# Reordering the first stretch of a fused attention and mixture kernel: who stores the head outputs, whose VectorE steps go first, how PSUM pairs rotate, and what is stored of the first expert's weights

## The chip, the cores and the metric

The kernel runs on one core of a Trainium2 chip. A core has a matrix engine (TensorE, PE in the profile; its weight loads are PEld), VectorE (DVE), ScalarE (ACT), GpSimd (POOL) and SyncE (SP), which here only issues DMA transfers. ScalarE can issue transfers too. Each engine executes its own instructions in order and waits on semaphores for the others. TensorE writes to eight PSUM banks of 128 x 512 floats; VectorE and ScalarE read them from there[...].

The time is the device time of the core in microseconds (us), from the first to the last instruction. All data is 32-bit float.

## The reference

First a causal linear attention with decay, 4 batches, 8 heads, 768 positions, head size 64. In blocks, for every head with its decay `lam`:

```python
intra = einsum('bhic,bhjc->bhij', qb, kb) * Dmask      # lam ** (i - j), lower triangle
intra = einsum('bhij,bhjd->bhid', intra, vb)
inter = einsum('bhid,bhde->bhie', qb * lam_pow, kv_state)
out[:, :, sl] = intra + inter
kv_state = lam_block * kv_state + einsum('bhsd,bhse->bhde', kb * rev_pow, vb)
```

The result, with the heads side by side, is x: 3072 tokens of width 512. Then four experts (512 to 1024 to 512), each token's outputs weighted by its normalised domain probabilities:

```python
p = domain_probs / (domain_probs.sum(-1, keepdims=True) + 1e-09)
for e in range(4):
    h = maximum(x @ w1[e], 0.0)
    out += p[:, e:e + 1] * (h @ w2[e])
```

## The kernel before

**Attention.** The sequence is cut into 24 chunks of 128 positions (six for each batch, all eight heads together). A chunk passes three steps of TensorE work, each with a pair of PSUM banks:

- `turn` (L494) transposes q and k (L500). ScalarE copies both out (qT L505, kT L506), VectorE makes qs, the decayed q, and GpSimd decays k in place for the state (`decayed`, kn in the profile).
- `scores` (L514) multiplies q and k of all heads (sp, L520). VectorE masks the two banks with the decays (two st of 128 x 512).
- `values` (L534) makes the outputs: from the state (L546, not in a batch's first chunk), from the masked scores (L551), and the new state's addend (L559, not in the last). ScalarE copies the outputs out (xc, L567), VectorE updates the state kv.

They are skewed: in turn i stand turn(i), scores(i-1), values(i-2). The pair of banks is chosen by the chunk's number modulo 3 (`pairs[n % 3]`), so all three steps of a chunk share a pair. `load` fetches q and k of four chunks ahead and v of three, in transfers of 128 and 256 KB whose rows are 64 floats.

**Experts.** Tokens are taken in three groups of 1024. Both matrix products of an expert use the Strassen-Winograd scheme: seven products of half-sized blocks (M1 to M7) in the place of eight, with sums of blocks as operands. For x times w1 it is nested: each of the seven products is done by seven inner ones. An inner product (L817, tile pg) is two 128x128 by 128x256 matmuls, four records in the profile; ScalarE or VectorE adds it up, and VectorE makes the sums hS of the hidden blocks for the second product (L871). A pair of group and expert is a unit; the seven products go in the order SEQ = M1, M5, M6, M2, M7, M3, M4. After the first unit's x-w1 part, TensorE interleaves the second product of one unit with the first of the next.

An operand tile of w1 is `ws_in`: 128 x 7 x 256 floats, four blocks and three further sums of them made by four GpSimd steps. There are two such buffers. For later use the operands of each expert are kept in DRAM: `w1_ops`, 896 KB for each of the seven products (`prepare_w1`, `inner`), and sums of w2 in `w2_sums` (`prepare_w2`). The x operands are `xs`: for the first group they stay in SBUF; for the other two the attention stage stores them to DRAM (`x_blocks`), both the plain head outputs (L574) and the block sums that GpSimd makes of a chunk and the one four before (`pair_sums`, tile to, L607).

**The first stretch**, which the change touches. `DENSE` = 14 turns of attention run alone; between them a list of chores (`chores`, started one at a time by `pump` when an estimate of GpSimd's load allows) fetches and completes the first expert's operands M1 and M5 (`own_fill`, `own_inner`, `own_sum`) and makes the w2 sums of expert 0. Then `first_product` does the seven products of the first unit; after each inner product `rest` gives VectorE one step from `background`, and `attend` issues attention steps at a rate (the rest spread over 35 inner steps). `own_fill` of the next product is called before a product begins; for S1 and S2 it is a ScalarE copy, for S3 and S4 two GpSimd subtractions, else a load. `own_inner` also stores each finished operand tile in five transfers, for the use of expert 0 in groups two and three.

Where the order comes from: `soon` puts attention's VectorE steps (qs, st, kv) in front of `background`, newest first; `values` settles those it still needs. A stored head output goes to the list `late` and is issued by SP two slots on; `store` does the like for GpSimd's results once its estimated load is through. SP's transfers are issued in the order of the program, and each waits for its data and for its buffer. In the program's semaphores a transfer also waits for the one eight before it in program order, whichever engine issued it.

```python
        if dense[0]:
            settle_up(what)
        else:
            background[0:0] = work
```

The functions below stand with the line numbers of the profile.

Of the kernel before, what the change touches and what calls it, by code (L numbers as in the profile page):

```python
# [22 lines left out]
def kernel(  # L23
# [11 lines left out]
    nc = tc.nc  # L35
# [289 lines left out]
    def own_fill(m):  # L325
        t = own[m] = stream.tile([P, 7, 256], FP32, name="ws_in", tag="w")
        a, blk = A_OF[m], whole(t)
        if a == "S3":
            halves(blk, raw["A11"][:], raw["A21"][:], ALU.subtract)
        elif a == "S4":  # L330
            halves(blk, raw["A12"][:], raw["S1"][:], ALU.subtract)
        elif a in ("S1", "S2"):
            nc.scalar.copy(out=blk, in_=raw["S1"][:])
        else:
            i, j = int(a[1]) - 1, int(a[2]) - 1
            nc.sync.dma_start(
                out=blk, in_=moe_w1[0, j * 256:(j + 1) * 256, i * W:(i + 1) * W].rearrange("(c p) f -> p c f", p=P),
            )

    def own_inner(m):  # L340
        t = own[m]
        for to, x, y, op in ((4, 0, 1, ALU.subtract), (1, 1, 3, ALU.add), (5, 1, 0, ALU.subtract), (6, 2, 5, ALU.subtract)):
            tt(nc.gpsimd, t[:, to], t[:, x], t[:, y], op)
        to = w1_ops[0, MS.index(m)]
        store(lambda: (
            nc.sync.dma_start(out=to[:, 0], in_=t[:, 0]),
            nc.sync.dma_start(out=to[:, 1:3], in_=t[:, 4:6]),
            nc.sync.dma_start(out=to[:, 3], in_=t[:, 1]),
            nc.sync.dma_start(out=to[:, 4], in_=t[:, 6]),
            nc.sync.dma_start(out=to[:, 5:7], in_=t[:, 2:4]),  # L350
            made.add(("w1", 0, m)),
        ))
        fed[0, 0, m] = {i: t[:, OWN_AT[i]] for i in OWN_AT}

    def own_sum(name):
        if name == "S1":
            raw["S1"] = stage.tile([P, 2, W], FP32, name="w1o", tag="st")
            halves(raw["S1"][:], raw["A21"][:], raw["A22"][:], ALU.add)
        else:
            halves(raw["S1"][:], raw["S1"][:], raw["A11"][:], ALU.subtract)  # L360
# [5 lines left out]
    for n, names in ((0, "qk"), (1, "qk"), (0, "v"), (2, "qk"), (1, "v"), (3, "qk"), (2, "v"), (3, "v")):  # L366
# [70 lines left out]
    background = []  # L437
    aside = []
# [26 lines left out]
    def soon(what, *work):  # L465
# [14 lines left out]
        else:  # L480
            background[0:0] = work
# [12 lines left out]
    def turn(n, tags):  # L494
# [39 lines left out]
    def values(n, tags):  # L534
# [37 lines left out]
        if g > 0:  # L572
            for r, m in plain.items():
                late.append((now[0] + 2, lambda r=r, m=m: nc.sync.dma_start(  # L574
                    out=x_blocks[g - 1, MS.index(m), :, :, at],
                    in_=x[:, r * 256:(r + 1) * 256].rearrange("p (a t) -> p a t", a=2),
                )))
# [37 lines left out]
    pairs = (("s0", "s1"), ("q01", "q02"), ("q11", "q12"))  # L615
# [6 lines left out]

    def attend():
# [453 lines left out]
    def nested_product(e, m, tags):  # L1077
# [45 lines left out]
    chores.extend((  # L1123
        lambda: (own_fill("M1"), raw_w1("A21", "A22")), pause(4),
# [158 lines left out]
```

## Time and profile before

The time is 1253.81 us, the median of two runs (1253.25 and 1254.37). The profiled execution spans 1251.8 us.

| engine | busy, us | share of the span | instructions |
|---|---|---|---|
| PE | 1197.9 | 96% | 6595 |
| PEld | 1036.8 | 83% | 6595 |
| DVE | 784.3 | 63% | 1330 |
| ACT | 286.7 | 23% | 522 |
| POOL | 630.4 | 50% | 628 |

The chain of work that ended last is 90% PE. Means of single steps, in the first 226 us: a mask st 682 ns, qs 862, an addition of an inner product 686, a decay kn 1087 on GpSimd, a head sum `to` 911 to 953, an operand step on ws_in 791; afterwards GpSimd's operand steps take about 0.72 us.

How to read it: a busy PE is not PE at its peak, because matmuls overlap and their ends are modelled. A mean over the span hides that the kernel has stretches with different limits, so the tables by stretch and the waits in one stretch count for more than the page's shares. The idle time of an engine that no one waits for costs nothing. The releaser of a wait is inferred; where the named one had long been done, it was another.

### The profile page before, as it was taken

To read this page: it belongs to the slowest core of one execution; us is meant where nothing else is said; L and a number is where in the kernel's file an instruction comes from. 1 tells how busy PE (TensorE), PEld (TensorE's weight loads), DVE (VectorE), ACT (ScalarE), POOL (GpSimd) and SP (SyncE) were. 2 spreads that over 40 slices of the span, in tenths; PEclk is the share of its full clock that TensorE was granted. 3 is DMA by queue.
4 is the path that set the end of the run, shared out by engine and by line. 5 is a ranking of instruction groups with operands and counts; after the bars stand their busy time and mean duration, and the time that the engine had idled before them with its cause. 6 is when DMAs were issued, how large, how long until landed. Compare 5 with 4: busy or idle time off the path is not lost.

```text
span 1251.8 us, 17937 instructions
## 1 busy us (share of the span) xinstructions
PE 1197.9 (96%) x6595; PEld 1036.8 (83%) x6595; DVE 784.3 (63%) x1330; ACT 286.7 (23%) x522; POOL 630.4 (50%) x628
## 2 busy tenths in 40 slices
PE   7888885999999999999999999999999999999998
PEld 6666663888888888888888888888888888888887
DVE  4744457278478467476476575575556566776775
ACT  3333222102102102012012022022124342242232
POOL 3468429757365422000721621467387486593784
PEclk9889989999999999999999999999999999999999
DMA  9978816987979644345675775767666535445442
GB/s 227 262 209 229 239 54 222 321 294 237 297 273 312 233 144 172 112 136 186 198 233 184 213 232 185 234 223 269 225 214 206 189 125 188 146 153 184 138 183 68
DMA packets 232390, 255.01 MB, mean 204 GB/s; under 512 B 95056, under 2 KB 185712, under 8 KB 232304
## 3 DMA queue, kind: packets, MB, share of 16 engines
q1 hardware_dynamic: 221696, 251.06, 62.9%
q10 hardware_dynamic: 10608, 2.82, 1.0%
q8 instruction: 52, 0.85, 0.3%
q14 instruction: 34, 0.28, 0.1%
HBM read 180.41 MB, written 73.42 MB: 203 GB/s over the span
## 4 chain that ended last, share of the span: by engine, by line
PE 90%; DVE 3%; DMA 2%; SPq 2%; POOL 1%; issue 1%; ACT 0%; ACTq 0%; DVEq 0%; POOLq 0%
PE pg L817 40%; PE q L871 31%; PE pq L1097 12%; PE op L551 2%; PE sp L520 2%; SPq L111 1%; PE kp L500 1%; PE op L546 1%; DVE st L76 1%; PE op L559 1%; DVE kv L76 0%; DVE m L76 0%; DVE sums L76 0%; DMA w_sums<-w2o 0%; PE qp L500 0%
## 5 line engine op out<-in xcount | busy, mean ns | idle before, releaser
L817 PE MATMUL pg<-xs,ws_in 128*128 128x256 f32 x2352 | 572.1, 382 | 14.7 <-DMA ws_in<-w_ops 10.3
L817 PEld LDWEIGHTS pg<-xs,ws_in 128*128 128x128 f32 x2352 | 445.5, 191 | 81.9 <-issue 11.3
L76 DVE TENSOR_TENSOR m<-pg,m 128x512 f32<-128x512 f32 x492 | 336.8, 688 | 146.9 <-PE pg L817 137.8
L871 PE MATMUL q<-w2t,hS 128*128 128x256 f32 x1024 | 241.9, 379 | 0.0
L871 PEld LDWEIGHTS q<-w2t,hS 128*128 128x128 f32 x1024 | 194.6, 190 | 26.5
L887 DVE SCALAR_TENSOR_TENSOR acc<-q,gate,acc 128x256 f32<-128x256 f32 x192 | 92.5, 482 | 160.3 <-PE q L871 160.0
L871 PE MATMUL q<-w2t,m 128*128 128x256 f32 x768 | 181.9, 379 | 0.3 <-DMA w2t<-in_moe_w_dram 0.2
L829 ACT ACTIVATE m<-m 128x512 f32<-128x512 f32 x144 | 90.7, 630 | 346.9 <-DVE m L76 346.7
L871 PEld LDWEIGHTS q<-w2t,m 128*128 128x128 f32 x768 | 146.0, 190 | 21.0 <-DMA w2t<-in_moe_w_dram 0.6
L76 POOL TENSOR_TENSOR ops<-w2b 128x256 f32<-128x256 f32 x24 | 16.9, 727 | 191.6 <-DMA w2b<-in_moe_w_dram 191.6
L76 POOL TENSOR_TENSOR m<-m,s_decay 128x512 f32<-128x512 f32 x64 | 80.4, 1273 | 63.0 <-ACT m L829 47.6
L76 POOL TENSOR_TENSOR xs<-xs 128x256 f32<-128x256 f32 x76 | 58.0, 764 | 107.2 <-DMA xs<-x_blocks 95.9
L825 ACT COPY m<-pg 128x512 f32<-128x512 f32 x96 | 56.2, 585 | 212.3 <-PE pg L817 192.2
L76 DVE TENSOR_TENSOR sums<-pq,sums 128x256 f32<-128x256 f32 x153 | 64.2, 422 | 46.0 <-PE pq L1097 35.8
L1097 PE MATMUL pq<-acc,w2t 128*128 128x256 f32 x352 | 86.6, 379 | 0.0
L1097 PEld LDWEIGHTS pq<-acc,w2t 128*128 128x128 f32 x352 | 66.8, 190 | 9.3 <-issue 0.3
L76 POOL TENSOR_TENSOR w2o<-w2b 128x512 f32<-128x512 f32 x32 | 41.5, 1317 | 59.4 <-DMA w2b<-in_moe_w_dram 21.7
L760 ACT ACTIVATE m<-m 128x512 f32<-128x512 f32 x48 | 30.3, 630 | 130.9 <-DVE m L76 130.9
L76 DVE TENSOR_TENSOR hS<-m,m 128x512 f32<-128x512 f32 x64 | 50.3, 786 | 15.4 <-ACT m L829 15.3
L76 POOL TENSOR_TENSOR acc<-hT,hT 128x512 f32<-128x512 f32 x32 | 40.3, 1272 | 30.1 <-PE pq L1097 28.2
L76 DVE TENSOR_TENSOR m<-m,m 128x512 f32<-128x512 f32 x64 | 53.6, 841 | 0.0
L76 POOL TENSOR_TENSOR acc<-hT,acc 128x512 f32<-128x512 f32 x32 | 40.6, 1270 | 7.4 <-PE pq L1097 5.4
(110 smaller groups left out, 1132.7 us busy)
## 6 DMA issues: line engine op xcount, KB each, us to landing
ws_in<-w_ops SPq DMA_DIRECT2D x77, 896.0 KB, 6.4
w2t<-w_ops SPq DMA_DIRECT2D x66, 256.0 KB, 5.0
w2t<-w_sums SPq DMA_DIRECT2D x64, 256.0 KB, 3.1
w2t<-in_moe_w_dram SPq DMA_DIRECT2D x48, 256.0 KB, 3.0
w_ops<-ops SPq DMA_DIRECT2D x21, 512.0 KB, 7.1
w1b<-in_moe_w_dram SPq DMA_DIRECT2D x16, 512.0 KB, 8.1
w2b<-in_moe_w_dram SPq DMA_DIRECT2D x32, 256.0 KB, 6.0
w_sums<-w2o SPq DMA_DIRECT2D x16, 512.0 KB, 8.8
```

The costliest lines, as they stand in the source:

```text
L76: eng.tensor_tensor(out=o, in0=a, in1=b, op=op)
L111: by.dma_start(out=to[:, :, r], in_=of[:, :, r])
L500: nc.tensor.transpose(out=x[:, ac * C:(ac + 1) * C], in_=y[:, 2 * ac:2 * ac + 2].rearrange("p r d -> p (r d)"), identity=ident[:],)
L520: nc.tensor.matmul(out=sp[r][:, ac * C:(ac + 1) * C], lhsT=hc(kT)[half[r], ac], rhs=hc(qT)[half[r], ac], start=True, stop=True,)
L551: nc.tensor.matmul(out=op[r][half[x], a * C:(a + 1) * C], lhsT=vn[:, 4 * r + 2 * a + x], rhs=hc(st[r])[:, 2 * a + x], start=(first and a = ...
L760: nc.scalar.activation(out=o[:], in_=o[:], func=AF.Relu)
L817: nc.tensor.matmul(out=p[:, j * 256:(j + 1) * 256], lhsT=ws[i][:, j * P:(j + 1) * P], rhs=xs[i], start=(fresh and j == 0), stop=True, skip ...
L825: nc.scalar.copy(out=new[at][:], in_=p[:])
L829: nc.scalar.activation(out=new[at][:], in_=new[at][:], func=AF.Relu)
L871: nc.tensor.matmul(out=p[:, s * DH:(s + 1) * DH], lhsT=h[A_OF[m]][:, c * 256 + s * P:c * 256 + (s + 1) * P], rhs=fed2[g, e, m][uu][:, c], ...
L887: nc.vector.scalar_tensor_tensor(out=o, in0=x, scalar=w, in1=o, op0=ALU.mult, op1=ALU.add)
L1097: nc.tensor.matmul(out=p[:, 0:256], lhsT=fed3[e, m, x // 2][:, x % 2, c * P:(c + 1) * P], rhs=b[B_OF[i]][:, c * 256:(c + 1) * 256], start= ...
```

## The change

Nothing of what is computed changes. Six edits belong together; they reorder the first stretch (attention and the first unit), and are meant to take waits out of it: transfers out of SP's queue, GpSimd's and VectorE's work out of the way of what TensorE needs next.

1. Head outputs of groups two and three are stored by ScalarE's queue, right after its copies, and no longer by SP two slots later.
2. Attention's VectorE steps go to a list of their own, `urgent`, taken oldest first, two after each inner product and one after each attention step, before the step from `background`.
3. PSUM pairs go round by step and not by chunk: four pairs while attention runs alone (the fourth is the one that the products use later), three afterwards. q and k are loaded five chunks ahead, v four.
4. The chores of the dense stage become a fixed table by turn (`early`); w1 blocks are fetched one at a time in turns 2 to 5; w2's sums of expert 0 move behind the dense stage, and `prepare_w1(1)` starts at the second product. Of the x operands of group one, VectorE now makes M1, M5 and M3 (before M1 and M2).
5. The first expert's w1 operands are not stored when they are made; `prepare_w1(0)` makes and stores them at the end of the list of chores, in time for group two. S3 and S4 are made in place in the raw blocks and copied by ScalarE like S1 and S2. `own_fill` of the next product comes after the first inner product, `own_inner` after the fifth.
6. A chunk's k is decayed in `scores`, one step later. The remaining attention is spread over 40 inner steps.

```diff
-        if a == "S3":
-            halves(blk, raw["A11"][:], raw["A21"][:], ALU.subtract)
-        elif a == "S4":
-            halves(blk, raw["A12"][:], raw["S1"][:], ALU.subtract)
-        elif a in ("S1", "S2"):
-            nc.scalar.copy(out=blk, in_=raw["S1"][:])
+        if a[0] == "S":
+            nc.scalar.copy(out=blk, in_=raw[{"S1": "S1", "S2": "S1", "S3": "A21", "S4": "A12"}[a]][:])
...
-        to = w1_ops[0, MS.index(m)]
-        store(lambda: (
-            nc.sync.dma_start(out=to[:, 0], in_=t[:, 0]),
...
-            made.add(("w1", 0, m)),
-        ))
...
-    for n, names in ((0, "qk"), (1, "qk"), (0, "v"), (2, "qk"), (1, "v"), (3, "qk"), (2, "v"), (3, "v")):
+    for n, names in ((0, "qk"), (1, "qk"), (0, "v"), (2, "qk"), (1, "v"), (3, "qk"), (2, "v"), (3, "v"), (4, "qk")):
...
-            background[0:0] = work
+            urgent.extend(work)
...
-        if n % NCH < NCH - 1:
-            decayed(kn)
 
     def scores(n, tags):
         qT, kT, _ = turned[n]
+        if n % NCH < NCH - 1:
+            decayed(nat[n, "k"])
...
-                late.append((now[0] + 2, lambda r=r, m=m: nc.sync.dma_start(
+                nc.scalar.dma_start(
...
-    pairs = (("s0", "s1"), ("q01", "q02"), ("q11", "q12"))
+    pairs = (("s0", "s1"), ("q01", "q02"), ("q11", "q12"), ("g1", "g3"))
...
-        f(n, pairs[n % 3])
+        f(n, pairs[next(turns) % (4 if dense[0] else 3)])
         if not attention or attention[0][0] != i:
+            if i + 5 < NT and i >= 0:
+                load(i + 5, "qk")
             if i + 4 < NT:
-                load(i + 4, "qk")
-            if 4 <= i + 3 < NT:
-                load(i + 3, "v")
+                load(i + 4, "v")
...
-    chores.extend((
-        lambda: (own_fill("M1"), raw_w1("A21", "A22")), pause(4),
-        lambda: own_inner("M1"), lambda: own_sum("S1"), lambda: (own_fill("M5"), raw_w1("A11")),
-        lambda: own_inner("M5"), lambda: own_sum("S2"),
-        *prepare_w2(0),
-    ))
+    early = {
+        2: (lambda: own_fill("M1"),), 3: (lambda: raw_w1("A21"),), 4: (lambda: raw_w1("A22"), lambda: own_inner("M1")),
+        5: (lambda: raw_w1("A11"),), 6: (lambda: own_sum("S1"),),
+        7: (lambda: own_fill("M5"), lambda: own_inner("M5")), 8: (lambda: own_sum("S2"),), 9: (lambda: own_sum("S3"),),
+        10: (lambda: x_inner(0, "M1", nc.vector), lambda: x_inner(0, "M6", nc.gpsimd), gates),
+        11: (lambda: x_inner(0, "M5", nc.vector), lambda: x_inner(0, "M2", nc.gpsimd)),
+        12: (lambda: x_inner(0, "M7", nc.gpsimd), lambda: x_inner(0, "M3", nc.vector)),
+        13: (lambda: x_inner(0, "M4", nc.gpsimd),),
+    }
...
-    rate = len(attention) / 35
+    rate = len(attention) / 40
...
-        if i > 0 and i < len(SEQ) - 1:
-            nxt = SEQ[i + 1]
-            own_fill(nxt)
-            chores.insert(0, lambda nxt=nxt: own_inner(nxt))
-            if nxt == "M2":
-                raw_w1("A12")
-            if nxt == "M7":
-                chores.extend(prepare_w1(1))
-        for f in first_product(0, 0, m, blocks, ("g1", "g3")):
+        if i == 0:
+            chores.extend(prepare_w2(0))
+        if i == 1:
+            chores.extend(prepare_w1(1))
+        for x, f in enumerate(first_product(0, 0, m, blocks, ("g1", "g3"))):
             f()
+            if 0 < i < len(SEQ) - 1:
+                if x == 0:
+                    own_fill(SEQ[i + 1])
+                    if i == 2:
+                        raw_w1("A12")
+                if x == 4:
+                    own_inner(SEQ[i + 1])
+                if i == 3 and x == 2:
+                    own_sum("S4")
             now[0] += 1
+            for _ in range(2):
+                take(urgent)
             rest()
             pump()
             credit += rate
             while credit >= 1 and attention:
                 credit -= 1
                 attend()
+                take(urgent)
...
-    chores.extend(prepare_w2(1) + prepare_w1(2) + prepare_w2(2) + prepare_w1(3) + prepare_w2(3))
+    chores.extend(prepare_w2(1) + prepare_w1(2) + prepare_w2(2) + prepare_w1(3) + prepare_w2(3) + prepare_w1(0))
```

More of the change, by code (lines that the diff above doesn't have):

```diff
@@ L343, in own_inner @@
             tt(nc.gpsimd, t[:, to], t[:, x], t[:, y], op)
-        to = w1_ops[0, MS.index(m)]
-        store(lambda: (
-            nc.sync.dma_start(out=to[:, 0], in_=t[:, 0]),
[L347 to L350, printed above, removed]
-            made.add(("w1", 0, m)),
-        ))
         fed[0, 0, m] = {i: t[:, OWN_AT[i]] for i in OWN_AT}
@@ L358, in own_sum @@
             halves(raw["S1"][:], raw["A21"][:], raw["A22"][:], ALU.add)
+        elif name == "S2":
+            halves(raw["S1"][:], raw["S1"][:], raw["A11"][:], ALU.subtract)
+        elif name == "S3":
+            halves(raw["A21"][:], raw["A11"][:], raw["A21"][:], ALU.subtract)
         else:
-            halves(raw["S1"][:], raw["S1"][:], raw["A11"][:], ALU.subtract)
+            halves(raw["A12"][:], raw["A12"][:], raw["S1"][:], ALU.subtract)
     fed = {}
@@ L437 @@
     background = []
+    urgent = []
     aside = []
@@ L573, in values @@
             for r, m in plain.items():
-                late.append((now[0] + 2, lambda r=r, m=m: nc.sync.dma_start(
+                nc.scalar.dma_start(
                     out=x_blocks[g - 1, MS.index(m), :, :, at],
                     in_=x[:, r * 256:(r + 1) * 256].rearrange("p (a t) -> p a t", a=2),
-                )))
+                )
         if not last:
@@ L621 @@
     ]
+    turns = itertools.count()
     def attend():
         i, f, n = attention.pop(0)
-        f(n, pairs[n % 3])
+        f(n, pairs[next(turns) % (4 if dense[0] else 3)])
         if not attention or attention[0][0] != i:
+            if i + 5 < NT and i >= 0:
+                load(i + 5, "qk")
             if i + 4 < NT:
-                load(i + 4, "qk")
-            if 4 <= i + 3 < NT:
-                load(i + 3, "v")
+                load(i + 4, "v")
         return i
@@ L1138 @@
             nc.scalar.dma_start(out=probs[:], in_=moe_domain_probs.rearrange("(t p) e -> p t e", p=P))
-        if i == 8:
-            gates()
-        if i > 9:
-            for m in SEQ[2 * (i - 10):2 * (i - 9)]:
-                x_inner(0, m, nc.vector if m in ("M1", "M2") else nc.gpsimd)
+        for f in early.get(i, ()):
+            f()
     dense[0] = False
-    for m in SEQ:
-        if ("x", 0, m) not in made:
-            x_inner(0, m, nc.gpsimd)
     blocks, credit = {}, 0.0
-    rate = len(attention) / 35
+    rate = len(attention) / 40
     for i, m in enumerate(SEQ):
@@ L1172 @@
                 attend()
+                take(urgent)
     while attention:
         attend()
+    while urgent:
+        take(urgent)
     fill3 = [(e, m, k) for e in range(E) for m in SEQ3 for k in range(4)]
```

## The prediction

> **What bounds the kernel now.** I read the page's slices first, then a table of stretches, then the waits of TensorE in the first 226 us, then the chain of work around the one long gap.
>
> ```profile
> ## 2 busy tenths in 40 slices
> PE   7888885999999999999999999999999999999998
>
> ```
>
> One digit is 31.3 us. From the eighth slice on TensorE is full; whatever can be won lies in the first seven. The stretches, cut at the first expert product (86.5), at the end of its last product (208.2) and at the restart (221):
>
> ```profile
> core 0: us, PE busy (x) PEld busy (x) DVE busy (x) ACT busy (x) POOL busy (x), PEclk, DMA share, GB/s
> 0.00:86.50 86.50, 66.49 (x863) 55.90 (x863) 50.92 (x101) 29.50 (x65) 37.85 (x42) 0.88 0.92 232
> 86.50:208.20 121.70, 102.36 (x966) 78.49 (x964) 68.86 (x109) 34.86 (x70) 73.28 (x83) 0.96 0.65 183
> 208.20:221.00 12.80, 2.25 (x9) 1.35 (x8) 4.30 (x5) 1.18 (x2) 12.41 (x14) 0.75 0.77 246
> 406.00:497.00 91.00, 91.00 (x423) 80.10 (x423) 57.92 (x96) 14.85 (x25) 26.75 (x30) 1.00 0.53 183
> ```
>
> From 221 a unit takes 91 us with TensorE busy for all of it: 1031 us that this change cannot shorten, only disturb. Before 221 no engine is full. At full clock the work of TensorE there is: transposes 0.44 for four, 48 fours, 21 us; scores 24 x 1.09 = 26; values 24 x 1.02 + 20 x (0.60 + 0.48) = 46; 49 inner products x 0.87 = 43; together 136 of 221 us. So 85 us are gaps, clock and operations measured longer than their best.
>
> ```profile
> PE pg L817 <- DMA ws_in<-w_ops: 10.3, 1, 10.3
> PE kp L500 <- DVE kv L76: 9.1, 11, 1.6
> PE op L546 <- DVE st L76: 7.8, 6, 1.7
> PE qp L500 <- DMA vn<-in_v_dram: 7.7, 1, 7.7
> PE op L559 <- POOL kn L76: 5.3, 1, 5.3
> PE kp L500 <- DVE kv L581: 2.8, 3, 1.7
> ```
>
> (total, times, longest). Three kinds: long single gaps, and two small ones that repeat each chunk. The 7.7 (23.1 to 30.8) has two causes: chunk 5's loads stand behind three 512 KB w1 loads in SP's order, and ScalarE, which must empty the PSUM banks, stands 8.6 us at the copy of S1 (L333) for GpSimd's sum. The 5.3 at 74.4: GpSimd waited 17.4 us for a store of w2 sums before it could reach the chunk's kn. The 10.3 is the end of this chain:
>
> ```profile
> 188.92 4.49 DMA ws_in<-in_moe_w_dram
> ...
> 199.10 3.46 POOL to L76 x3
> ...
> 206.33 4.85 DMA w2t<-in_moe_w_dram
> 211.19 4.46 DMA w_ops<-w1b
> 215.78 5.14 DMA ws_in<-w_ops
> ```
>
> M4's operand is fetched when M7 has freed its buffer, GpSimd completes it, then makes the last head sums, only then expert 1's first operand; that is stored and read back, and TensorE waits.
>
> **What the Trainium skill says.** "TensorE: Matmul & The Clock Gate", section HAM oscillation: idle gaps over some 3.4 us drop the clock to half. The trace agrees: after the 7.7 us gap the mean granted clock is 0.62 in 30.8 to 39, and a score step takes 2.01 instead of 1.09. "Perfetto Trace Analysis", section Matmuls: independent groups should rotate through PSUM banks so that evacuation overlaps; the 14 waits of kp for kv are the lack of this. "DMA: Bandwidth & Descriptors", section Issuing engines are not separate DMA queues: another issuing engine saves issue time only. The DMA share of 0.92 with 232 GB/s to 86.5 says the same: moving stores does not make room. "GPSIMD Engine Reference", section 1, Specifications: its SBUF interfaces are shared with VectorE where that reads two SBUF inputs. Here such a VectorE step takes 0.42 alone and 1.28 beside a GpSimd step.
>
> **The change part by part.**
>
> *w1 operands of expert 0 not stored, w2 sums after the dense stage, w1 blocks fetched in turns 2 to 5.* In the dense stage this takes out 1.8 MB of stores and some 2 MB of w2 loads and more of w2 sums. At 205 GB/s (the mean of 187 and 222 in the first two stretches of 10 us) chunk 5's q and k, now 4.2 MB into the queue instead of 5.8, land at 20.5 us, before TensorE asks at 23. The S1 copy comes three turns later than before, behind a sum already made. Gain: the 7.7, and the slow clock behind it (qp, kp, sp, op took 5.2 instead of 2.9: 2.3). The store that held GpSimd moves out: gain the 5.3 and its slow clock (qp, kp, sp at 4.1 instead of 2.0: 2.1).
>
> *Four PSUM pairs, taken by turn.* A turn no longer takes the pair that values has just left. That removes kp's waits: 3.8 + 1.7 before 86.5, 5.3 + 1.0 after. In the dense stage VectorE is nearly full at chunks 4 to 7 (9.73 of 10 us at 50 to 60, with qs, two st, kv and four head sums: 4.5 to 5.6 us per turn against 4.1 of TensorE), so I take half: 2.7. Outside of it there are three pairs, now one for each kind of step; all 6.3 count.
>
> *VectorE's attention steps oldest first.* The second mask st was put behind the next chunk's; L546 then waited 1.7 us each time. Gain 7.8; the hidden part is that one product add moves back by 0.7, which TensorE does not feel while its two banks alternate.
>
> *Head outputs stored by ScalarE.* 24 stores x about 0.6 us of issue is 14 us on an engine busy 35 of 122; SP loses as much and no longer waits 35.2 us for L567. Cost at nothing, hidden under ScalarE's idle time, if its waits are short. Each DMA waits in the built program for the DMA eight before it, so a store can hold ScalarE, and behind it the bank copies qT, kT and xc for TensorE. Bound: nothing, to one 3.3 us landing for each of 24, 79 us. The DMA eight back is a load or store of about one chunk earlier, 5 us old against 3.3 us; I take nothing, and keep part of it below.
>
> *kn's decay one step later* is needed a step later still; hidden. The third VectorE operand step (4 x 0.42) trades for one of GpSimd's; nothing.
>
> *New waits.* M2's fill stands on SP behind chunk 15's head store by the lane rule, and on GpSimd behind two w2 sums (5 us) that wait for a w2 store issued after it. From the end of chunk 15's values: landing 5, issue 2, store 6, sums 5, operand 3: 21 us, against 15 to 18 us of TensorE work: 0 to 7, I take 4. M4's operand stands on GpSimd behind the sums of chunks 21 to 23 (3 x 4 us): 0 to 6, I take 3; VectorE's 25 additions for M3 and M4 (0.68 to 0.75 each, 18 us against 12 of TensorE) set that stretch in both kernels anyway. Longer SP and GpSimd queues in the dense stage (operand of M1 at turn 4, GpSimd 4.2 us per turn at 10 to 13): 0 to 6, I take 3.
>
> *Expert 1.* w1's preparation starts one product earlier, and M1 of expert 1 is stored before M4's fill, so the chain above loses GpSimd's step, store and landing: of 10.6 lost, 1 remains. But GpSimd now starts M5, M7, M6, M2, M3 about 6 us later relative to TensorE. In the order of SP, M6's load stands behind M3's store: GpSimd 27 us after its last head sum, issue 5, landing 7: 39, against TensorE's need at 36. Cost 3, range 0 to 8.
>
> *Expert 0's operands prepared later for the second group.* 28 inner steps of 0.73 and 8 halves of 1.25 are 31 us of GpSimd, with 2.1 MB loaded and 6.4 MB stored, in 406 to 497. GpSimd has 27 of 91 us there and the DMA share is 0.53 at 183 GB/s; 8.5 MB are 93 GB/s more. In SP's order each store stands five products or more ahead of its read. Cost: nothing, hidden under 91 us of TensorE.
>
> *Sum.* Dense stage: 86.5 - 7.7 - 2.3 - 5.3 - 2.1 - 2.7 + 3 = 69.4. Second stage: 121.7 - 7.8 - 6.3 - half of the lost clock (0.04 x 121.7 / 2 = 2.4) + 4 + 3 = 112.2. Restart: 12.8 less the 2.2 us of work in it is 10.6, now 1, and M6's 3. Old 86.5 + 121.7 + 10.6 = 218.8; new 69.4 + 112.2 + 4 = 185.6. Gain 33: 1254 - 33 = 1221.
>
> **The rivals.** *A, half of it.* The dense stage is at a DMA share of 0.92, and if it stays bound by loads it ends at 76; M2's, M4's and M6's waits come in at their ends (7 + 6 + 8 instead of 10). 1221 + 7 + 11 = 1239. For: q, k and v come in 256-byte rows at little over 200 GB/s. Against: 3.8 MB leave the stage. *B, the second stage flows better.* 136 us of work in 186 still leaves 50; if VectorE's order also removes half of the long ScalarE waits for op and the new waits stay hidden (10 less), and 7 us more of clock: 1204. *C, slower.* ScalarE's stores hold its copies for 2 us each at 24 places (48 us), all new waits at their ends (+11), or expert 0's late operands stall the second group: 1221 + 48 + 11 = 1280. For: ScalarE executes in order, and four of the 24 DMAs eight back are SP transfers that themselves wait for GpSimd. Against: those are a chunk old, and SP itself no longer waits for ScalarE.
>
> **How the numbers follow.** Forecast 0.62 (1210 to 1230), A 0.18 (1230 to 1250), B 0.15 (below 1210), C 0.05 (above 1250). I predict 1220. Eight in ten: 1202 to 1242, which takes in B's and A's points and the ends of the new waits. The 2% bounds are 1228.7 and 1278.9: faster is B and nearly all of the forecast, 0.75; within 2% is A, the forecast's upper end and the mild part of C, 0.21; slower 0.04.
>
> **What would show it.** First product at 66 to 76 us; no wait of qp over 3 us for a load; kp's waits for kv gone and L546's for st below 2 us in all; GpSimd not held 17 us by a w2 store before the first product. The gap before the second unit is under 4 us, and TensorE runs full from about 186. Between M6 and M2 and before M4 gaps of 3 to 5 us, the first released by GpSimd's operand. Units of 91 us after that, the third with GpSimd near 58 us and a DMA share near 0.8. Wrong would be: ScalarE idle for DMA landings in front of qT and xc; a dense stage above 78; TensorE waits in the units after the restart.

## The result and the profile after

The changed kernel takes 1222.64 us, the median of two runs (1222.17 and 1223.12), against 1253.81 before: ratio 0.9751, 95% interval 0.971 to 0.9793. The prediction of 1220 was 2.6 us short; the gain is 31.2 us where it said 33. That close a sum hides two errors of 11 to 12 us with opposite signs, so the steps matter more than the total.

In the changed kernel the lines have moved: L811 is L817 of before (an inner product), L865 is L871, L492 is L500 (a transpose), L512 is L520 (scores), L538, L543 and L551 are L546, L551 and L559 (the three parts of values), L559 is ScalarE's copy xc. First the page's slices of the changed kernel, now 30.5 us each:

```profile
PE   9589898999999999999999999999999999999998
...
PEclk9899999999999999999999999999999999999999
```

TensorE is full from the eighth slice on, as before. The seventh, where the gap at the restart stood at 5, is now at 8: the gap is gone, and a wait at M6 of expert 1 has come. The second slice (30.5 to 61) is down to 5, where the kernel before had 8. The stretches of the changed kernel, cut at the same events as before (first expert product, end of the first unit's last product, restart), with the third unit after the restart last:

```profile
core 0: us, PE busy (x) PEld busy (x) DVE busy (x) ACT busy (x) POOL busy (x), PEclk, DMA share, GB/s
0.00:81.20 81.20, 62.57 (x863) 54.00 (x863) 61.14 (x102) 28.52 (x65) 41.95 (x48) 0.92 0.91 210
81.20:182.28 101.08, 94.93 (x965) 74.94 (x966) 75.77 (x113) 35.42 (x71) 77.81 (x81) 0.98 0.74 210
182.28:184.75 2.47, 1.89 (x9) 1.35 (x8) 1.60 (x3) 1.26 (x2) 2.47 (x3) 1.00 1.00 406
...
369.70:460.70 91.00, 91.00 (x423) 80.12 (x422) 57.82 (x93) 14.82 (x25) 55.48 (x63) 1.00 0.76 257
```

| part | before | predicted | after |
|---|---|---|---|
| dense stage | 86.5 | 69.4 | 81.2 |
| second stage | 121.7 | 112.2 | 101.1 |
| lost at the restart | 10.6 | 1 | 0.6 (2.47 less 1.89 of work) |
| wait at M6 of expert 1 | none | 3 | 3.9 |
| sum | 218.8 | 185.6 | 186.8 |

The waits of TensorE in the first 226 us of the changed kernel (total, times, longest):

```profile
PE op L538 <- DVE kv L76: 9.0, 3, 5.6
PE op L551 <- POOL kn L76: 6.5, 2, 5.6
PE pg L811 <- DMA ws_in<-w_ops: 4.5, 2, 3.9
PE pg L811 <- DVE m L76: 3.5, 6, 1.2
PE pg L811 <- POOL ws_in L76: 2.5, 1, 2.5
...
PE qp L492 <- DMA qn<-in_q_dram: 0.5, 1, 0.5
```

The waits named for removal are gone: the transposes' waits for kv (9.1 and 2.8), the output products' for the mask (7.8), the 7.7 for a load, the 5.3 for kn at 74.4, and nearly all of the 10.3 at the restart. What is new stands first: waits of the output products for kv and of the state's addend for kn, 5.6 us each at the longest, all in the dense stage. In numbers, TensorE is idle for 18.6 of the 81.2 us there, hardly less than the 20.0 of before; 16.5 us of that are the new waits.

The 3.9 us for a stored operand are M6 of expert 1 (start, duration, in brackets the wait):

```profile
214.78 2.47 PE L811 MATMUL pg<-xs,ws_in 128*128 128x256 f32 x8 [3.88 <-DMA ws_in<-w_ops]
```

Of the late operands in the second stage, M2's is on the chain of work of the changed kernel (start, duration, what):

```profile
110.86 4.56 DMA x_blocks<-xc
...
115.44 5.20 DMA ws_in<-in_moe_w_dram
...
126.06 3.27 POOL w2o L76 x2
129.32 1.14 POOL ws_in L76
```

That is the chain the prediction wrote down (head store, fill, w2 sums, operand). It cost TensorE 2.5 us.

**Where the dense stage's two gaps come from.** GpSimd's timeline in the changed kernel (start, duration, operation, and in brackets the idle time before it with its releaser):

```profile
32.31 3.13 POOL L76 TENSOR_TENSOR ws_in<-ws_in 128x256 f32<-128x256 f32 x4 [14.98 <-DMA ws_in<-in_moe_w_dram]
35.40 1.05 POOL L76 TENSOR_TENSOR kn<-kn,s_decay 128x512 f32<-128x512 f32 x1
...
52.02 2.87 POOL L76 TENSOR_TENSOR w1o<-w1o,w1b 128x512 f32<-128x512 f32 x2
...
56.05 3.12 POOL L76 TENSOR_TENSOR w1b<-w1b 128x512 f32<-128x512 f32 x2
```

GpSimd stood 15 us at M1's load, which lands at 32.3; the chunk's kn came behind it at 36.5, and TensorE stood from 30.9 to 36.5. Twenty us later GpSimd makes the sums S2 and S3. VectorE's timeline there:

```profile
53.68 1.49 DVE L76 TENSOR_TENSOR xs<-xc 128x256 f32<-128x256 f32 x1
...
56.29 1.75 DVE L76 TENSOR_TENSOR qs<-qT,q_decay 128x512 f32<-128x512 f32 x1
...
59.16 1.30 DVE L76 TENSOR_TENSOR kv<-kv,q_decay 128x256 f32<-128x256 f32 x1
60.60 0.42 DVE L76 TENSOR_TENSOR kv<-kv,op 128x256 f32<-128x256 f32 x1
60.94 0.42 DVE L76 TENSOR_TENSOR xs<-xc 128x256 f32<-128x256 f32 x1
```

A head sum takes 1.23 to 1.49 us while GpSimd works, and 0.42 right after GpSimd's last step has ended at 60.2. VectorE has no pause of more than 0.2 us here, and TensorE waits from 55.5 to 61.1 for the kv at its end. Whether these two readings are causes was for the experiments.

### The profile page after: what moved, and what is told of

It reads as the page before. It is cut to its first block, busy times and chain, and to the rows that moved or that the text cites. A ratio compares the mean times of both kernels' runs of the same rounds, so it can differ in the third digit from the quotient of the medians.

```text
span 1220.4 us, 17976 instructions
## 1 busy us (share of the span) xinstructions
PE 1186.7 (97%) x6595; PEld 1030.8 (84%) x6595; DVE 796.9 (65%) x1334; ACT 286.4 (23%) x524; POOL 663.3 (54%) x660
## 4 chain that ended last, share of the span: by engine, by line
PE 89%; DMA 4%; DVE 4%; POOL 2%; issue 0%; SPq 0%; ACT 0%; ACTq 0%; DVEq 0%
PE pg L811 40%; PE q L865 31%; PE pq L1091 13%; PE op L543 1%; DMA ws_in<-w_ops 1%; DMA qn<-in_q_dram 1%; PE sp L512 1%; DMA ws_in<-in_moe_w_dram 1%; PE op L538 1%; DVE m L76 1%; DVE xs L76 1%; DVE qs L76 1%; POOL w2o L76 1%; DVE st L76 1%; DVE hS L76 0%
## 5 line engine op out<-in xcount | busy, mean ns | idle before, releaser
L811 PE MATMUL pg<-xs,ws_in 128*128 128x256 f32 x2352 | 569.9, 381 | 10.7 <-DMA ws_in<-w_ops 4.5
L811 PEld LDWEIGHTS pg<-xs,ws_in 128*128 128x128 f32 x2352 | 443.0, 190 | 78.3 <-DVE m L76 8.3
L865 PE MATMUL q<-w2t,hS 128*128 128x256 f32 x1024 | 243.1, 380 | 0.0
L865 PEld LDWEIGHTS q<-w2t,hS 128*128 128x128 f32 x1024 | 195.6, 191 | 27.0
L865 PE MATMUL q<-w2t,m 128*128 128x256 f32 x768 | 181.4, 379 | 0.0
L865 PEld LDWEIGHTS q<-w2t,m 128*128 128x128 f32 x768 | 145.9, 190 | 19.8
L76 DVE TENSOR_TENSOR hS<-m,m 128x512 f32<-128x512 f32 x64 | 50.9, 795 | 15.4 <-ACT m L823 15.3
L76 DVE TENSOR_TENSOR m<-m,m 128x512 f32<-128x512 f32 x64 | 50.3, 786 | 0.0
```

The costliest lines, as they stand in the source:

```text
L76: eng.tensor_tensor(out=o, in0=a, in1=b, op=op)
L811: nc.tensor.matmul(out=p[:, j * 256:(j + 1) * 256], lhsT=ws[i][:, j * P:(j + 1) * P], rhs=xs[i], start=(fresh and j == 0), stop=True, skip ...
L865: nc.tensor.matmul(out=p[:, s * DH:(s + 1) * DH], lhsT=h[A_OF[m]][:, c * 256 + s * P:c * 256 + (s + 1) * P], rhs=fed2[g, e, m][uu][:, c], ...
```

## The experiments

Each ratio is against the kernel before on the same chip. "First product" is the end of the dense stage. The stages and waits come from one profiled execution of each kernel. The interval of the change itself is wide, as it had two runs only; u2, which turned out like it in every stage, serves as a second measure of it.

| label | ratio, 95% interval | median, us | first product | second stage | waits for w1 operands after it |
|---|---|---|---|---|---|
| the change | 0.9751, 0.971 to 0.9793 | 1222.6 | 81.2 | 101.1 | M2 2.5, M6 3.9, restart 0.6 |
| u1_pairs | 0.9781, 0.9762 to 0.98 | 1226.4 | 86.3 | 101.2 | 3.0 in all |
| u2_newest | 0.9751, 0.9731 to 0.977 | 1222.3 | 81.1 | 101.2 | 2.7 and 4.6 |
| u4_w1_stored | 0.978, 0.9761 to 0.98 | 1226.2 | 81.2 | 105.1 | M2 6.4, restart 3.8 |
| d1_m1_later | 0.9702, 0.9686 to 0.9717 | 1216.7 | 75.6 | 101.8 | 3.0 and 3.1 |
| u3_sp_stores | 0.9736, 0.9714 to 0.9759 | 1220.6 | 80.7 | 100.9 | 2.3 and 4.6 |
| u5_one_step | 0.9801, 0.9783 to 0.9818 | 1229.5 | 82.3 | 110.2 | 2.3 |
| d3_no_sums | 0.97, 0.9679 to 0.972 | 1217.2 | 73.4 | 105.8 | 4.3 and 3.4 |
| d4_sums_later | 0.9696, 0.9679 to 0.9714 | 1216.6 | 73.8 | 99.4 | restart 6.0 |
| b2_steps | 0.9833, 0.9811 to 0.9855 | 1231.7 | 86.2 | 101.7 | restart 10.1 |
| v1_sp_probs | 0.9719, 0.9695 to 0.9743 | 1217.9 | 73.6 | 100.8 | restart 8.7 |
| v3_w1_first | 0.9727, 0.9705 to 0.9748 | 1218.2 | 71.1 | 101.5 | 2.2 and 7.8 |
| v5_w2_vector | 0.9742, 0.9728 to 0.9755 | 1222.3 | 74.4 | 104.7 | 2.4 and restart 7.3 |

### One edit undone at a time

**u1_pairs.** PSUM pairs by chunk again.

```diff
-        f(n, pairs[next(turns) % (4 if dense[0] else 3)])
+        f(n, pairs[n % 3])
```

> The changed kernel with one edit undone: a chunk again keeps one pair of PSUM banks for its three steps (pair by chunk number modulo 3). If the prediction's sum is right, kp waits for kv come back: 2.7 us in the dense stage and 6.3 after it, so about 1229 to 1232 (changed kernel 1222.6). Rival: the first 81 us are set by VectorE and GpSimd, and oldest-first VectorE steps already bring kv early, so the pairs are worth 0 to 3: 1222 to 1226.

The median is 3.7 us up, just above the rival's range and below the prediction's; the intervals of the two kernels overlap, so the stages have to decide, and they fit neither text. The waits of this kernel up to its first product, and its second stage:

```profile
PE kp L492 <- DVE kv L76: 9.3, 8, 4.0
```

```profile
86.25:187.45 101.20, 95.16 (x966) 75.26 (x965) 76.12 (x111) 35.75 (x71) 78.53 (x81) 0.98 0.74 213
```

In the dense stage the pairs are worth 5 us (86.3 against 81.2), not 2.7; after it they are worth nothing, not 6.3. In the second stage kv is nearly always ready before the next transpose asks for the pair: the waits of kp for kv are 1.6 us there, with pairs by chunk.

**u2_newest.** Newest steps first, the two takes after each inner product kept.

```diff
-            urgent.extend(work)
+            urgent[0:0] = work
```

> The changed kernel with attention's VectorE steps put at the front of their list again (newest first), the two steps taken after each inner product kept. If the order is what removed the 7.8 us of output products waiting for the second mask, those waits come back: 1228 to 1231. Rival: what removed them is the number of steps taken (two after each inner product instead of one), the list is nearly always empty and the order is worth 0 to 2: 1222 to 1225.

No difference: 0.9751, second stage 101.2. The order of the list, which the prediction priced at 7.8 us, is worth nothing as long as two steps are taken after each product.

**u5_one_step.** The order kept, the number of takes cut to that of before.

```diff
-            for _ in range(2):
-                take(urgent)
-            rest()
+            urgent[:] = [f for f in urgent if not f.over]
+            take(urgent) if urgent else rest()
...
                 attend()
-                take(urgent)
```

> The changed kernel, VectorE's attention steps still oldest first, but one VectorE step after each inner product (attention's if there is one, else background), and none after an attention step, as many as before. Theory N, the number of steps taken is what removed the waits of the output products for the second mask (undoing the order alone cost nothing): waits of op for st of 5 to 8 us come back in the second stage, second stage 107 to 112 instead of 101, total 1228 to 1234. Rival, the order was enough and either of the two removes them: 1221 to 1225.

```profile
PE op L538 <- DVE kv L76: 6.0, 3, 2.9
82.30:192.45 110.15, 98.21 (x966) 77.33 (x965) 69.61 (x108) 35.67 (x71) 80.17 (x85) 0.97 0.73 213
```

The second stage grows by 9.1 us, as theory N said, and the time by 7. The waits that come back are others than it named: 6.0 for kv instead of the mask. So the number of steps counts, with the order kept. What the order is worth with one step after each product was not tested: with one step and newest first the kernel before has 121.7, but it differs in the other edits too.

**b2_steps.** The kernel before with this edit alone (list, order and number).

```diff
-            background[0:0] = work
+            urgent.extend(work)
...
+            for _ in range(2):
+                take(urgent)
             rest()
...
                 attend()
+                take(urgent)
```

> The kernel before with the edit of VectorE's steps alone: attention's steps in a list of their own, oldest first, two after each inner product and one after each attention step, before the one from background. Theory N: this edit alone takes out the waits for the second mask (8.7 us) and, since kv comes earlier, the waits of kp for kv in the second stage (6.3 us) too, second stage 104 to 109 instead of 121.7, dense stage unchanged at 86.5, total 1236 to 1242. Rival G: GpSimd's chain to expert 1's first operand sets the restart, so what the second stage wins is lost in front of the restart (wait 15 us or more instead of 10.3), total 1246 to 1253.

The first two stretches of this kernel, and its waits of kp for kv after the first:

```profile
0.00:86.23 86.23, 65.61 (x862) 54.90 (x862) 52.11 (x101) 29.55 (x65) 36.76 (x41) 0.88 0.92 232
86.23:187.93 101.70, 94.04 (x966) 73.52 (x965) 74.60 (x111) 35.39 (x71) 75.57 (x85) 1.00 0.78 220
PE kp L501 <- DVE kv L76: 1.5, 2, 1.1
```

It beats its own theory: 1231.7, and the second stage shrinks from 121.7 to 101.7, nearly the whole of what the change wins there. The waits for the mask are gone, and those of kp for kv are 1.8 us instead of 6.3, with the pairs still by chunk. Idle time of TensorE falls from 19.3 to 7.7 us, and its busy time from 102.4 to 94.0 for the same 966 matmuls, at a mean clock of 1.00 instead of 0.96. The dense stage and the restart stay as before (86.2; wait 10.1), so rival G, that the restart takes the gain back, is out. Alone, this edit brings 21.5 us; all six bring 31.2.

**u3_sp_stores.** Head outputs issued by SP again, two slots later.

```diff
-                nc.scalar.dma_start(
+                late.append((now[0] + 2, lambda r=r, m=m: nc.sync.dma_start(
...
```

> The changed kernel with the head outputs of groups two and three issued by SP again, two slots after the copies. Prediction's reading, who issues is worth nothing in itself: 1220 to 1226, with M2's operand a little later because SP again waits for the copies. Rival: the second stage is 11 us shorter than predicted because SP no longer stands at ScalarE's copies (35 us of waits before): second stage 105 to 112 instead of 101, total 1227 to 1233.

0.9736, inside the interval of the change, and all stages within 0.5 us but the restart, where 2.8 us are lost instead of 0.6. Who issues the stores is worth nothing that was measured; the second stage is not shorter because SP no longer stands at ScalarE's copies.

**u4_w1_stored.** The first expert's operands stored when made, five transfers each, and `prepare_w1(0)` dropped from the end of the chores.

```diff
         fed[0, 0, m] = {i: t[:, OWN_AT[i]] for i in OWN_AT}
+        to = w1_ops[0, MS.index(m)]
+        store(lambda: (
+            nc.sync.dma_start(out=to[:, 0], in_=t[:, 0]),
...
-    chores.extend(prepare_w2(1) + prepare_w1(2) + prepare_w2(2) + prepare_w1(3) + prepare_w2(3) + prepare_w1(0))
+    chores.extend(prepare_w2(1) + prepare_w1(2) + prepare_w2(2) + prepare_w1(3) + prepare_w2(3))
```

> The changed kernel, but the first expert's w1 operands are stored when they are made, as before, and not made again at the end of the chores. Prediction's reading, the first 81 us limited by transfers: the 1.8 MB of M1 and M5 stored there cost 5 to 9 us, the 4.6 MB after it 0 to 3: 1228 to 1234. Rival, the first 81 us are limited by GpSimd and VectorE and not by transfers: stage end within 2 us of 81, total 1221 to 1226.

Here are its first two stretches:

```profile
0.00:81.18 81.18, 62.93 (x863) 53.92 (x863) 60.45 (x102) 28.55 (x65) 42.70 (x48) 0.92 0.95 227
81.18:186.25 105.07, 94.95 (x966) 74.99 (x965) 74.89 (x113) 35.61 (x71) 77.45 (x81) 0.97 0.83 243
```

The dense stage moves 227 GB/s instead of 210 and ends at the same 81.2, as the rival said. So these stores do not set its end, and taking 1.8 MB out of it bought nothing in this kernel. (They come after the load at which GpSimd stands from 17 to 32; of that load they say nothing.) The stores cost later: M2's operand 6.4 us late instead of 2.5, the restart 3.8 instead of 0.6. From the restart to the end it takes 1030.8 us against 1035.7, and 3.9 of those 4.9 are M6's wait, which this kernel has not: the late preparation of expert 0's operands costs about 1 us at most.

### The dense stage

**d1_m1_later.** GpSimd's steps one to two turns later, all loads as they were.

```diff
-        2: (lambda: own_fill("M1"),), 3: (lambda: raw_w1("A21"),), 4: (lambda: raw_w1("A22"), lambda: own_inner("M1")),
-        5: (lambda: raw_w1("A11"),), 6: (lambda: own_sum("S1"),),
-        7: (lambda: own_fill("M5"), lambda: own_inner("M5")), 8: (lambda: own_sum("S2"),), 9: (lambda: own_sum("S3"),),
+        2: (lambda: own_fill("M1"),), 3: (lambda: raw_w1("A21"),), 4: (lambda: raw_w1("A22"),),
+        5: (lambda: raw_w1("A11"),), 6: (lambda: own_inner("M1"),), 7: (lambda: own_sum("S1"),),
+        8: (lambda: own_fill("M5"), lambda: own_inner("M5")), 9: (lambda: own_sum("S2"), lambda: own_sum("S3")),
```

> The changed kernel with GpSimd's steps on the first expert's operands one to two turns later: M1 after turn 6 instead of 4, the S1 sum after 7, M5 after 8, S2 and S3 after 9, loads as they were. Theory G: the dense stage ends 12 us later than predicted because GpSimd stands 15 and 7 us at two loads with a decay of k behind it; without that the 5.6 us gap at 31 and its slow clock go, first expert product at 73 to 76 instead of 81, total 1214 to 1217. Rival L: the loads set the stage (DMA share 0.9 to 1.0), waits of the transposes for q and k take the gap's place, stage end 79 to 82, total 1220 to 1223. Rival V: VectorE from chunk 4 on sets it, the gap at 55 grows by what the first lost, same numbers as L but VectorE busy 9.9 of 10 us and no waits for loads.

```profile
PE op L538 <- DVE kv L76: 8.3, 4, 4.7
...
PE sp L512 <- ACT kT L498: 2.8, 1, 2.8
PE op L551 <- POOL kn L76: 2.4, 1, 2.4
```

Theory G holds: first product at 75.6, total 1216.7, both within its numbers, and no wait for q or k over 0.5 us. Measured beside u2 on the same chip it is 5.6 us faster, and the intervals of these two do not touch. This kernel also shows the next limit. VectorE's head sums, one with GpSimd idle (from 37 to 44.8) and one beside its sums S2 and S3:

```profile
41.28 0.42 DVE L76 TENSOR_TENSOR xs<-xc,xs 128x256 f32<-128x256 f32 x1
...
55.03 1.48 DVE L76 TENSOR_TENSOR xs<-xc,xs 128x256 f32<-128x256 f32 x1
```

**d3_no_sums** takes GpSimd's steps out of that place (the diff is against d1). S1, S2 and S3 are left out, so the first unit's M5, M6, M7 and, through S4, M3 multiply other blocks; M5's four steps move to the start of the products.

```diff
-        5: (lambda: raw_w1("A11"),), 6: (lambda: own_inner("M1"),), 7: (lambda: own_sum("S1"),),
-        8: (lambda: own_fill("M5"), lambda: own_inner("M5")), 9: (lambda: own_sum("S2"), lambda: own_sum("S3")),
+        5: (lambda: raw_w1("A11"),), 6: (lambda: own_inner("M1"),), 7: (lambda: raw.update(S1=raw["A22"]),),
+        8: (lambda: own_fill("M5"),),
...
             chores.extend(prepare_w2(0))
+            own_inner("M5")
```

> The kernel with GpSimd's M1 steps after turn 6 (1216.7), with the w1 sums S1, S2 and S3 left out (the plain blocks stand in their place, so M5, M6 and M7 of the first unit multiply other numbers) and M5's four GpSimd steps moved to the start of the products. GpSimd then has only decays in turns 7 to 9. Theory V, VectorE's steps on two SBUF inputs take 1.2 to 1.5 us beside GpSimd and 0.42 alone and set the stage from 48 to 61: head sums, qs and kv there at 0.42, 0.69 and 0.55, the waits of op for kv (8.3) down to 2 to 3, first product at 68 to 71 instead of 75.6, total 1208 to 1212. Rival L, the loads take over: waits of qp or kp for q and k of 4 to 6 us, first product 74 to 76, total 1214 to 1217.

```profile
PE sp L512 <- ACT kT L498: 7.0, 2, 3.6
PE op L538 <- DVE kv L76: 1.6, 2, 1.0
```

The waits for kv fall from 8.3 to 1.6, and head sums that took 1.2 to 1.5 us take 0.42 in most cases, so theory V is right about its cause. The stage still ends only 2.3 us earlier, at 73.4, because another wait takes the place: sp for kT, 7.0 us in two. ScalarE's timeline at the later one:

```profile
59.21 1.37 ACTq L566 DMA_DIRECT2D x_blocks<-xc  x2
60.67 0.58 ACT L497 COPY qT<-qp 128x512 f32<-128x512 f32 x1 [7.90 <-DMA kn<-in_k_dram]
```

By the profile ScalarE stood 7.9 us: its two head stores were issued only when a k load had landed, and qT and kT stood behind them. This is the mechanism of rival C, and it shows as soon as TensorE runs ahead. The other place is the load of the domain probabilities (L1135), which ScalarE also issues; in the changed kernel it holds ScalarE for 6.2 us too, but that lies under the gap at kn. What d3 won in front it lost behind: its second stage is 105.8, with M2's operand 4.3 us late, so the total is that of d1.

**d4_sums_later** is a whole computation with the same aim: M1 and S1 as in d1 (the diff is against it), M5's steps and S2 at the start of the products, S3 in the third.

```diff
-        8: (lambda: own_fill("M5"), lambda: own_inner("M5")), 9: (lambda: own_sum("S2"), lambda: own_sum("S3")),
+        8: (lambda: own_fill("M5"),),
...
-            chores.extend(prepare_w2(0))
+            chores.extend([pause(12)] + prepare_w2(0))
+            own_inner("M5")
+            own_sum("S2")
...
+                if i == 2 and x == 2:
+                    own_sum("S3")
```

> As a whole computation: GpSimd's M1 steps after turn 6, S1 after 7, but M5's four steps and S2 at the start of the products, S3 in the third product (w2's sums start 12 slots later). Theory V: GpSimd has one sum only in turns 7 to 9, dense stage ends at 70 to 73; M5's steps and S2 (6 us) lie in GpSimd's free 6 to 9 us before its first head sum. Total 1209 to 1214, if the second stage stays at 101 to 103. Rival: GpSimd, 78 of 101 us busy in the second stage, pays it back there: M2's and M6's waits grow by what is won, total 1215 to 1219.

The dense stage ends at 73.8, a little later than theory V said, and the second stage takes 99.4, less than it said. This run also bears on d3's reading: S1 is kept, and with S2, S3 and M5's steps gone from that place the longest wait for kv there falls from 4.7 us (d1) to 0.5. A wait of 3.7 us remains one chunk later, where VectorE and GpSimd make x operands side by side and four VectorE steps take 3.4 us. The total is 1216.6 all the same, as the rival said, but at another place than it named: M2 no longer waits, and the restart waits 6.0 us for expert 1's first operand.

**v1_sp_probs** is d4 with the probabilities issued by SP, and the head stores too, by the edit of u3.

```diff
-            nc.scalar.dma_start(out=probs[:], in_=moe_domain_probs.rearrange("(t p) e -> p t e", p=P))
+            nc.sync.dma_start(out=probs[:], in_=moe_domain_probs.rearrange("(t p) e -> p t e", p=P))
```

> The kernel with M1's steps after turn 6 and M5's steps and S2, S3 after the dense stage (1216.6), and besides the head outputs and the load of the domain probabilities issued by SP and no longer by ScalarE. Theory A: ScalarE, standing at such an issue for a k load to land (4.4 and 6 to 8 us), holds qT and kT for TensorE; without it the wait of sp for kT (4.0) goes, dense stage 69 to 72 instead of 73.8. Total 1211 to 1216, since GpSimd's chain to expert 1's first operand (no pause from 109 to 190) gives part of it back at the restart. Rival L: the late k load itself is the bound and the transposes wait for it directly: dense stage 73 to 75, total 1216 to 1218.

The wait of sp for kT is gone, and the stage still ends at 73.6: the transposes now wait for k and q themselves (2.1 and 0.7), ScalarE stands 7.1 us at the copy of S1, for GpSimd's sum, and kn and kv are waited for (2.7 and 4.4). Theory A was right about ScalarE and wrong about the gain. L had the number, but the loads are the smaller part of what takes the place. The total is 1217.9.

### What holds the total at 1217

Five kernels with a dense stage of 71 to 76 us (d1, d3, d4, v1 and v3) end between 1216.6 and 1218.2. In each of them TensorE waits 3 to 9 us for expert 1's stored operands.

**v3_w1_first.** v1 with the first eight steps of expert 1's w1 preparation ahead of expert 0's w2 sums.

```diff
-            chores.extend([pause(12)] + prepare_w2(0))
...
+            w1_steps = prepare_w1(1)
+            chores.extend([pause(12)] + w1_steps[:8])
         if i == 1:
-            chores.extend(prepare_w1(1))
+            chores.extend(prepare_w2(0) + w1_steps[8:])
```

> As the run with SP's stores and probabilities, and the first eight steps of expert 1's w1 preparation come before expert 0's w2 sums in GpSimd's order (11 us of w2 sums move behind). Theory: GpSimd's order sets the restart and M6's wait; with it the waits for stored w1 operands (6 us together) go to under 2, total 1206 to 1211. Rival: GpSimd's total work is the bound, the wait moves to M7's or M6's w2 sums or operands in the second unit: total 1212 to 1217.

```profile
195.26 3.75 PE L811 MATMUL pg<-xs,ws_in 128*128 128x256 f32 x8 [7.79 <-DMA ws_in<-w_ops]
```

The restart no longer waits, and the product after it, M5, waits 7.8 us for its stored operand. The wait moved, as the rival said, though to M5, which it did not name; the total of 1218.2 is just above its range. The chain of work in front of this wait (start, duration, what) shows the reason:

```profile
183.92 2.95 DMA w_sums<-w2o
...
187.27 0.42 SPq L846
...
187.75 7.37 DMA ws_in<-w_ops
```

M5's load stands in SP's queue behind loads of expert 0's w2 sums (L846), and these wait for the sums to be made and stored, which the new order put late: GpSimd makes them from 181.4, after standing 8.3 us for a store. So here it is an order again, of SP's queue and of the w2 sums. Whether GpSimd's total work sets the restart in d4, the next run asks.

**v5_w2_vector.** d4 with expert 0's w2 sums on VectorE.

```diff
+            if e == 0:
...
+                for i in range(2):
+                    tt(nc.vector, o[:, i], x[:, i], y[:, i], op)
...
+            else:
+                halves(*parts, op)
```

> The kernel with M1's steps after turn 6 and M5's steps, S2 and S3 after the dense stage (1216.6; first product at 73.8, restart 6 us late), and expert 0's w2 sums made by VectorE and no longer by GpSimd, 8 steps of 128x512. Theory G: GpSimd, without a pause from 109 to 190, now sets the restart, which is why five kernels with dense stages of 71 to 76 all end at 1216.6 to 1218.2; with 11 us less on it the waits for stored w1 operands (6.0) fall below 2 and the end comes to 1209 to 1213, VectorE going from 80 to 86 to 90 us of the second stage. Rival V: VectorE, 80 of 99 us busy, is as near to its limit: waits of pg for m grow from 5 to over 10, total 1215 to 1220.

Theory G fell. GpSimd's load in the second stage went from 80.6 of 99.4 us to 66.6 of 104.7, and the restart wait grew from 6.0 to 7.3. GpSimd's timeline in this kernel:

```profile
160.35 0.73 POOL L76 TENSOR_TENSOR to<-xc 128x256 f32<-128x256 f32 x1 [6.27 <-ACT xc L567]
...
169.43 3.64 POOL L76 TENSOR_TENSOR ws_in<-ws_in 128x256 f32<-128x256 f32 x4
...
176.66 1.41 POOL L76 TENSOR_TENSOR ops<-w1b 128x256 f32<-128x256 f32 x2
```

GpSimd stands 6.3 us for a head output before 160. Then the head sums of the last chunks come together with M4's operand, and expert 1's first operand is begun behind them at 176.7, to be stored and read back by 188. So the amount of GpSimd's work is not the limit at the restart. That the first operand stands behind the last chunks' sums fits better: in v3 GpSimd begins it at 126.3, ahead of those sums, and the restart has no wait. But v3 differs from this kernel in the w2 sums too; no run changed that order by itself. TensorE's waits for VectorE's m (4.7 us) did not grow as rival V said; the total of 1222.3 is above the ranges of both. Why the second stage itself is 5.3 us longer than in d4 stays open too.

## Why the prediction was right, step by step

- *Which stretch can be won.* Right. Units after the restart take 91 us; the third, which carries the late preparation of expert 0's operands, runs at 91.0 with GpSimd at 55.5 and a DMA share of 0.76 (predicted: near 58 and 0.8).
- *By its own signs.* The first product was to come at 66 to 76 us, and a dense stage above 78 was named as a sign of being wrong. It came at 81.2, so by that sign the account of the dense stage was wrong, although the total was right. Another sign came too: ScalarE stands 6.2 us for a k load in front of qT, which here lies under the wait for kn. Of the signs after the dense stage, the short restart and the units of 91 us came as written; the gap at M2 is 2.5 us where 3 to 5 were named, and before M4 there is none.
- *w1 operands not stored, w2 sums later, w1 blocks in turns 2 to 5: -7.7, -2.3, -5.3, -2.1.* Both named waits went, and TensorE's busy time fell by 3.9 us (66.5 to 62.6), near the 4.4 allowed for the clock. But the stage got only 5.3 us shorter, and by u1 the pairs alone are worth 5.0. The 17 us were taken back by the new waits, with a slow clock behind the two long ones (0.76 in 30 to 40, 0.70 in 60 to 70). The stores do not set the stage's end: u4 puts them back and it does not move. Removing two waits of one chain is not the sum of them when another in-order queue is about as late.
- *New waits of the dense stage: +3.* This is the step that failed: the new waits are 16.5 us, against a range of 0 to 6. "Operand of M1 at turn 4" was named; undoing it is worth 5.6 us of the stage (d1). That GpSimd's w1 sums, now in turns 6 to 9, would slow VectorE was not priced at all, although the prediction drew on the Trainium skill, "GPSIMD Engine Reference", section 1, Specifications, which says that GpSimd and VectorE share SBUF interfaces and contend when VectorE has two SBUF inputs, and it had 0.42 and 1.28 us beside each other. The trace agrees with the page (1.23 to 1.49 us beside GpSimd, 0.42 after it). VectorE's busy time rose from 50.9 to 61.1 us in a shorter stage, though four of its operand steps are new; with GpSimd's sums out of the way, d1's 8.3 us of waits for kv fall to 1.6 (d3).
- *Four pairs: -2.7 and -6.3.* 5.0 and 0 (u1). VectorE being nearly full was no reason to halve the first. The second was won by the VectorE steps: in b2, with pairs by chunk, the waits of kp for kv are already down from 6.3 to 1.8.
- *Oldest first: -7.8.* The waits went, but the mechanism was mis-named. With two steps a product the order is worth 0 (u2), the number of steps is worth 9.1 with the order kept (u5), and both together 20.0 on the kernel before (b2).
- *Slow clock in the second stage: -2.4.* TensorE's busy time for the same matmuls fell by 7.4 (102.4 to 94.9). I took half of the lost clock, and left out that parts of `values` overlap more when none of them waits. The 160 state products alone went from 9.7 to 6.7 us busy, before and after, while the mean of one hardly moved:

```profile
L546 PE MATMUL op<-qs,kv 64*64 64x128 f32 x160 | 9.7, 288 | 8.6 <-DVE st L76 7.8 <-DVE kv L76 0.9
L538 PE MATMUL op<-qs,kv 64*64 64x128 f32 x160 | 6.7, 282 | 0.0
```

- *New waits of the second stage: +4 and +3.* 2.5 and none. M2's chain was the one predicted; before M4 there is no such wait. So of the 11 us by which the second stage beat the forecast, 5.0 are busy time and 4.5 waits that did not come; the rest is small waits.
- *Restart 1, M6 3.* 0.6 and 3.9, right in size. M6's load leaves SP's queue at 207.3, after stores of GpSimd's results and four loads of w2 blocks, and lands at 214.6; no run tested which of these holds it.
- *ScalarE's stores at nothing.* Right for this kernel (u3). The Trainium skill, "DMA: Bandwidth & Descriptors", section Issuing engines are not separate DMA queues, says that another issuing engine saves only the time of issue, and the runs agree: with SP as issuer the stages stay within 0.5 us except the restart. The bound was not idle, though: d3 shows ScalarE standing 7.9 us at such a store once TensorE no longer waits elsewhere.
- *Rivals.* B's mechanism (the second stage flows better) and A's outcome (the dense stage does not reach 69) both happened, 11 to 12 us each, and cancelled. A's reason, loads, was not what held the changed kernel: d1 keeps all loads and wins 5.6 us. That the time was 1222.6 is in large part the luck of that sum.

The fastest kernels here that compute everything are the change with GpSimd's w1 steps one to two turns later (d1, 0.9702) and its variant d4 (0.9696), 6 us below the change and 38 below the kernel before.

## What to carry to other kernels

When steps are inserted by hand into an in-order engine, count how many are taken per slot before asking in which order: too small a number cost 9 us here, and with enough of them the order was worth nothing. Before subtracting a wait from a stage, look for the next queue that is equally late, above all an engine standing at a load with a small urgent step behind it. And when work is moved to GpSimd because it is idle at that moment, price what its steps do to VectorE's: here a step on two SBUF inputs went from 0.42 to as much as 1.49 us.

## What was not expected of the hardware

- Beside GpSimd's sums a VectorE step with two SBUF inputs takes up to three and a half times as long: head sum 0.42 to 1.49 us, decay of kv 0.42 to 1.30, qs 0.69 to 1.75. Steps with one input in PSUM do not change: two masks 1.27 to 1.28, the addition to kv 0.42, beside GpSimd too. GpSimd loses less: a decay of k takes 1.24 instead of 1.06.
- A transfer that ScalarE issues held its ordinary work for 7.9 us (a head store, d3) and 6.2 us (the load of the probabilities, changed kernel), by the profile until a transfer of other data, a k load, had landed. Elsewhere such stores cost nothing visible (u3).
- The same 966 matmuls of the second stage are 102.4 us of busy TensorE with 19.3 us of gaps, none over 2 us, and a mean clock of 0.96, and 94.0 us with 7.7 us of gaps and a mean clock of 1.00 (b2).
